# An attention and mixture-of-experts chain on one core: the order of the opening's ropes, of the zeros' transfers and of the jobs' hand-overs

## The chip, the cores and the metric

The kernel runs on one core of a Trainium2 chip. The core has five engines with a program each: TensorE (PE; matmuls and transposes, with the weight loads, PEld, beside them), VectorE (DVE), ScalarE (ACT), GpSimd (POOL) and SyncE (SP), which here only issues transfers (DMA). Each engine works through its own instructions in order and waits for others by semaphores. The metric is the device time of one execution in microseconds (us); lower is better.

## The reference

Three layers in a row, all in float32 as seen from outside; w_in and w_out come as float64 and are turned into float32 pairs on the chip.

```python
q_rot, k_rot = rotate(q), rotate(k)                    # rope; 2 batches, 8 heads, 576 tokens, 64 wide
scores = scale * q_rot @ k_rot.T
attn = exp(scores - max); attn /= sum(attn)
x = (attn @ v), as 1152 tokens x 512

expert = argmax(x @ w_gate)                            # 8 experts, at most 288 tokens kept for each
out[i] = gate_w[i] * (relu(x[i] @ w1[expert]) @ w2[expert])   # 512 -> 1024 -> 512; dropped tokens are 0

h = out @ w_in                                         # 512 -> 2048
g = max(h, 0) + alpha * min(h, 0)
result = g @ w_out                                     # 2048 -> 512
```

## The kernel before, in words

The order of all work is written out by hand (`tc.manual_schedule()`): each engine executes its instructions in the order in which the Python code emits them, and the framework adds the waits. So a call that is moved in the code moves its instructions on every engine that it uses, and nowhere else.

**Attention** (`attention`) works on eight pairs of heads, j = 0 to 7. For a pair it loads k, q and v (`prep_load`), rotates k and q (`ropeA`: three tensor_tensor instructions, two products and a sum; `remA`: the same for the last 64 of the 576 tokens), splits them into a high and a low half (`ropeB`: a rounding on ScalarE and a subtraction; `remB`), transposes them (`prep_T`, `prep_rem`) and copies the result crosswise by DMA (`prep_X`, tile X). `S_step(j, t, hh)` is a block of scores: matmuls on TensorE, the row maximum on VectorE (tile nm), the exponential on ScalarE (tile P). `T_step` transposes a P, and ScalarE or VectorE copies it out of PSUM (tile PT); `AV_steps` multiplies by v (av, then oT). Pair 0 goes a shorter way without halves: `first_T` transposes its rotated q or k for one head (tiles fT, then first), `first_rem` its last 64 tokens (frem). `warm(k)` issues k matmuls on zeros whose result nobody reads. V is VectorE, Q is GpSimd in these calls; H0 and H1 are the first and the second head of the pair. The opening, up to the loop over n at line 501, is a list of such calls; the loop does ten steps n for a pair, and `hook(n)` at the end of a step does other layers' work.

**Zeros.** From n = 17 on, `hook` issues one transfer of zeros (96 x 3 x 512 floats, 576 KB) in each step: nine into x_disp, the buffer of dispatched tokens, and four into out. They go through SP's queue, like the loads of q, k and v and the copies into X. `prep_load(j + 3)` stands in the last step of a pair, so k of pair 5 is loaded at n = 29 and rotated by GpSimd at n = 30.

**The experts** are taken by size (rank r = 0, 1, ...). The first two (r < NSTAT) are done by `job`, in nine steps s: 24 matmuls a step, half of them to h (relu, then split by ScalarE into a high and by VectorE into a low half), half into the four accumulators acc. Between these, `job(r)` splits its own weights and those of rank r + 1 (`split`: ScalarE rounds, VectorE subtracts; tiles wraw to whl), issues the loads of rank r + 1 on SP (`load`, `load_xs`), and transposes rank r + 1's tokens (`turn_x`, `make_xT`; tiles xs, xt, then split_room or x32). `job(1)` also splits the first float64 weights of the last layer (`split_w_in`, five instructions for each quarter; tiles rawy and room) and loads the next ones (`load_w_in`). After the two jobs the program branches; the way taken here (`short_way`) does ranks 2, 3 and 4 in float32 with `mid_job` (160 columns) and `small_job` (32 columns each), in which `next_x` turns the next rank's tokens and loads those of the one after. Before the change the fourth rank's tokens (r = 3) are loaded at the start of `mid_job`, behind the loads of rank 3's second and third weights.

**The last layer** (`ffn`) then runs over three blocks of 272, 256 and 256 columns, and the results are scattered to out by GpSimd.

Of the kernel before, what the change touches and what calls it, by code (L numbers as in the profile page):

```python
# [37 lines left out]
NSTAT = 2  # L38
WS = 192
USE = (0, 2, 1, 3)  # L40
SIZES = (32, 64, 128, 160, 192, W)
FIT = (W, W, 160, 32, 32)
# [21 lines left out]
def attention(nc, tc, q, k, v, wg, tab, rtab, x_tok, lp, ident, idr, hook):  # L64
# [3 lines left out]
    with ExitStack() as ctx:  # L68
# [372 lines left out]
        H0, H1 = (0, 1), (1, 2)  # L441
# [5 lines left out]
        ropeA(0, Q, 1, H1)  # L447
        remA(0, V)
        first_T(1, 0)
        first_T(0, 0)  # L450
# [6 lines left out]
        remA(1, Q)  # L457
        first_T(0, 1, nc.vector)
        T_step(0, 0, 0)
        S_step(0, 2, 0)  # L460
        prep_sums(1)
        ropeA(1, Q, 0)
        S_step(0, 0, 1)
        prep_load(2)
        remB(1, V)
        ropeB(1, Q, 1)
        ropeA(2, Q, 1)
        T_step(0, 0, 1)
        ropeB(1, V, 0)
        T_step(0, 1, 0)  # L470
        T_step(0, 2, 0)
        prep_load(3)
# [9 lines left out]
        T_step(0, 3, 0)  # L482
        prep_T(1, 0, 1)
        T_step(0, 2, 1)
# [363 lines left out]
def build(nc, tc, cap, q, k, v, wg, w1, w2, w_in, w_out, alpha, tab, rtab, out):  # L848
    assert 0 < cap <= W
    with ExitStack() as top:  # L850
# [113 lines left out]
        def hook(n, psum):  # L964
# [12 lines left out]
            if n > 16 and fill:  # L977
                nc.sync.dma_start(fill.pop(0), zero[0:96].unsqueeze(1).broadcast_to([96, 3, 512]))
# [24 lines left out]
        with ExitStack() as ctx:  # L1003
# [235 lines left out]
            with ExitStack() as c1:  # L1239
# [45 lines left out]
                def job(r, base, nxt):  # L1285
# [13 lines left out]
                    for s in range(9):  # L1299
# [40 lines left out]
                        for chore in chores.pop((r, s), ()):  # L1340
                            chore()
                        if r < NSTAT:
                            if s in ((0, 1) if r else (1, 2)):
                                split(r, 2, ((0, 1), (2, 3))[s - (r == 0)], lo)
                            if s in (3, 4):
                                split(r, 3, part, lo)
                            if s in (2, 5) and nxt:
                                load(r + 1, 2 + s // 4)
# [16 lines left out]
                        if nxt:  # L1365
# [4 lines left out]
                            for c in ({3: (0,), 5: (1,), 6: (2,), 7: (3,)} if r else {6: (0, 1), 7: (2, 3)}).get(s, ()):  # L1370
                                if r + 1 == NSTAT:
                                    nc.scalar.copy(x32[:, c], turn_x(r + 1, c, ph, "xt")[:, 0:WS])
                                    continue
                                src = make_xT(r + 1, c, ph, "xt")
                                if r + 1 > NSTAT:
                                    nc.vector.tensor_copy(x32[:, c], src[:, 0:WS])
# [8 lines left out]
                        if r == 1 and s in (2, 4):  # L1385
                            load_w_in(1, 2 - s // 2)
# [73 lines left out]
                def mid_job(r, base, nxt, n, nx=None):  # L1460

                    h = [h32[:, f * n : f * n + n] for f in range(8)]
                    if nxt and r == NSTAT:
                        load_xs(r + 1, nx or n)
# [84 lines left out]
                for r in range(NSTAT):  # L1549
                    job(r, None if r else 0, True)  # L1550
                load(NSTAT + 1, 2)
# [110 lines left out]
```

## Time and profile before

| | us |
|---|---|
| median of three runs | 418.86 |
| the three runs | 418.72, 422.13, 418.86 |
| the profiled execution, its own time | 422.35 |
| its span, first to last instruction | 420.6 |
| mean granted TensorE clock in it | 0.989 |

| engine | busy us | share of the span |
|---|---|---|
| TensorE | 394.2 | 94% |
| VectorE | 284.6 | 68% |
| ScalarE | 225.4 | 54% |
| GpSimd | 137.2 | 33% |

TensorE is busy nearly all the time. So the place to read is not the share of an engine but the places where TensorE waits, and for each of them which engine or transfer ended the wait. The profiled execution is one execution, and its own time is nearer to the slowest of the three runs than to their median.

### The profile page before, as it was taken

To read this page: it belongs to the slowest core of one execution; us is meant where nothing else is said; L and a number is where in the kernel's file an instruction comes from. 1 tells how busy PE (TensorE), PEld (TensorE's weight loads), DVE (VectorE), ACT (ScalarE), POOL (GpSimd) and SP (SyncE) were. 2 spreads that over 40 slices of the span, in tenths; PEclk is the share of its full clock that TensorE was granted. 3 is DMA by queue.
4 is the path that set the end of the run, shared out by engine and by line. 5 is a ranking of instruction groups with operands and counts; after the bars stand their busy time and mean duration, and the time that the engine had idled before them with its cause. 6 is when DMAs were issued, how large, how long until landed. Compare 5 with 4: busy or idle time off the path is not lost. (4 is left out here: it accounts for less than half of the span.)

```text
span 420.6 us, 8109 instructions
## 1 busy us (share of the span) xinstructions
PE 394.2 (94%) x2999; PEld 334.9 (80%) x2999; DVE 284.6 (68%) x643; ACT 225.4 (54%) x565; POOL 137.2 (33%) x180
## 2 busy tenths in 40 slices
PE   5899999989999999999898889899999999999994
PEld 2577888777978777799798887699799789879873
DVE  6566566465877465688698802199999999983621
ACT  7587787578867687447634411176327415622500
POOL 5899594499496333250000071000000000000032
PEclk9799999999999999999999999999999999999998
DMA  7622999905023631857957598940550253000022
GB/s 211 167 60 61 165 349 303 275 7 133 1 58 114 207 106 46 292 182 244 319 183 265 200 316 270 397 158 2 200 201 2 70 201 132 2 0 2 0 77 81
DMA packets 37328, 63.70 MB, mean 151 GB/s; under 512 B 9886, under 2 KB 16158, under 8 KB 37280
## 3 DMA queue, kind: packets, MB, share of 16 engines
q1 hardware_dynamic: 35424, 58.83, 44.1%
q0 software_dynamic: 1568, 3.95, 2.6%
q8 instruction: 25, 0.41, 0.4%
q10 hardware_dynamic: 288, 0.33, 0.2%
q14 instruction: 23, 0.19, 0.1%
HBM read 47.35 MB, written 11.65 MB: 140 GB/s over the span
## 5 line engine op out<-in xcount | busy, mean ns | idle before, releaser
L309 DVE TENSOR_REDUCE nm<-S 128x1 f32<-128x576 f32 x72 | 54.2, 753 | 39.0 <-ACT PT L320 20.6
L1135 PE MATMUL u_a<-yh,whl 128*128 128x256 f32 (+1 forms) x576 | 71.1, 284 | 0.6 <-ACT yh L1457 0.4
L1135 PEld LDWEIGHTS u_a<-yh,whl 128*128 128x128 f32 x576 | 70.1, 188 | 1.8 <-ACT room L1145 0.9
L310 ACT ACTIVATE P<-S,nm 128x576 f32<-128x576 f32 x72 | 53.7, 746 | 24.5 <-DVE nm L309 23.1
L596 POOL DMA_INDIRECT out<-xs,room x3 | 2.9, 974 | 150.3 <-DVE xs L1211 150.3
L331 PE MATMUL pt<-ident,P 128*128 128x128 f32 x256 | 39.0, 277 | 3.6 <-ACT P L310 2.0
L1199 PE MATMUL acc<-whl,split_room 128*128 128x512 f32 x162 | 41.5, 392 | 0.0
L1029 ACT CAST whl<-wraw 128x512 fp32r<-128x512 f32 x22 | 14.6, 662 | 48.9 <-DVE wraw L1027 48.9
L300 PE MATMUL S<-T,T 128*128 128x288 f32 x112 | 36.4, 341 | 1.2 <-ACT P L310 0.9
L1199 PEld LDWEIGHTS acc<-whl,split_room 128*128 128x128 f32 x162 | 29.9, 188 | 9.4 <-issue 2.6
L320 ACT COPY PT<-pt 128x512 f32<-128x512 f32 x64 | 35.4, 557 | 2.2 <-PE pt L331 2.2
L331 PEld LDWEIGHTS pt<-ident,P 128*128 128x128 f32 x256 | 28.7, 141 | 8.9 <-ACT P L310 3.7
L363 PE MATMUL av<-PT,v 128*64 128x288 f32 x256 | 34.8, 412 | 0.0
L1199 PE MATMUL acc<-whl,g 128*128 128x512 f32 x126 | 32.6, 390 | 0.0
L300 PE MATMUL S<-X,T 128*128 128x288 f32 x112 | 31.2, 293 | 0.0
L1146 DVE SCALAR_TENSOR_TENSOR room<-room,nal 128x256 f32<-128x256 f32 (+1 forms) x48 | 23.4, 487 | 8.9 <-ACT room L1145 8.7
L1199 PEld LDWEIGHTS acc<-whl,g 128*128 128x128 f32 x126 | 23.5, 188 | 5.7 <-issue 0.9
L596 POOL DMA_INDIRECT meta_d<-g_meta,m_mi x10 | 9.6, 961 | 56.1 <-DVE m_mi L839 53.4
L1144 ACT ACTIVATE room<-u_a 128x256 f32<-128x256 f32 (+1 forms) x48 | 19.0, 396 | 15.5 <-PE u_a L1135 15.5
L363 PEld LDWEIGHTS av<-PT,v 128*64 128x64 f32 x256 | 17.2, 136 | 12.0 <-issue 1.9
L300 PEld LDWEIGHTS S<-T,T 128*128 128x128 f32 x112 | 21.1, 188 | 3.0 <-ACT P L310 2.5
L136 POOL TENSOR_TENSOR A<-raw,tabt 128x512 f32<-128x512 f32 (+1 forms) x15 | 19.1, 1276 | 9.5 <-DMA raw<-k 9.1
(288 smaller groups left out, 853.5 us busy)
## 6 DMA issues: line engine op xcount, KB each, us to landing
wraw<-moe_w SPq DMA_DIRECT2D x16, 1024.0 KB, 7.0
wraw<-moe_w_out SPq DMA_DIRECT2D x3, 2048.0 KB, 8.1
x_disp<-zero SPq DMA_DIRECT2D x9, 576.0 KB, 7.2
wraw<-moe_w_in SPq DMA_DIRECT2D x2, 2048.0 KB, 7.5
X<-T SPq DMA_DIRECT2D x14, 288.0 KB, 5.5
room<-moe_w SPq DMA_DIRECT2D x3, 1024.0 KB, 7.6
out<-zero SPq DMA_DIRECT2D x4, 576.0 KB, 7.8
v<-v SPq DMA_DIRECT2D x8, 256.0 KB, 4.4
```

The costliest lines, as they stand in the source:

```text
L136: eng.tensor_tensor(A, raw, bc(C), op=ALU.mult)
L300: nc.tensor.matmul(ps[:, half, 0:288], lhsT=lhsT, rhs=rhs, start=(n == 0), stop=(n == len(terms) - 1),)
L309: nc.vector.tensor_reduce(nm, ps[:, :, 0:288], op=ALU.max, axis=AX.XY, negate=True)
L310: nc.scalar.activation(Pt.rearrange("p (a n) -> p a n", a=2), ps[:, :, 0:288], AF.Exp, bias=nm, scale=1.0, accum_out=st["ssum"][:, t, hh : ...
L320: (nc.vector.tensor_copy if SCH["e"][k] else nc.scalar.copy)(o, i)
L331: nc.tensor.transpose(ps[:, kb, :], Pt[:, at : at + 128], ident)
L363: nc.tensor.matmul(ps[64 * hh : 64 * hh + 64, 0:288], lhsT=lhs, rhs=(PT[:, hh, kb] if kb < 4 else PR)[:, half * 288 : half * 288 + 288], s ...
L1029: nc.scalar.copy(ht[:, 0, c], hw.bitcast(F32))
L1135: nc.tensor.matmul(ps, lhsT=wt[:, a, c, (f % 4) * 128 : (f % 4) * 128 + 128], rhs=yh_[0][:, b, c, c0 + lo : c0 + hi], start=(c == 0 and i ...
L1144: nc.scalar.activation(A, ps, AF.Relu)
L1146: nc.vector.scalar_tensor_tensor(A, Bn, nal[:, f : f + 1], A, op0=ALU.mult, op1=ALU.add)
L1199: nc.tensor.matmul(ps[:m], lhsT=g_cols(g, b, t * P, t * P + m), rhs=wt[:, a, c, :], start=(c == 0 and i == 0), stop=(c == 3 and i == 2),)
```

## The change

In the opening the second half of pair 0's k goes from GpSimd to VectorE, behind the rope of the remaining tokens (`remA(0, V)`); two warm matmuls are added; GpSimd's `remA(1, Q)` and the order of some transposes and copies change. The zeros are issued at every second step. In `job`, the next rank's tokens are transposed and copied ahead of the splits and loads of the same step, and the second load of float64 weights goes ahead of the other loads. The load of rank 3's tokens goes from the start of `mid_job` to the end of the second job, ahead of two weight loads.

```diff
         ropeA(0, V, 1, H0)
         ropeA(0, V, 0, H0)
-        ropeA(0, Q, 1, H1)
         remA(0, V)
         first_T(1, 0)
+        ropeA(0, V, 1, H1)
+        warm(2)
         first_T(0, 0)
         first_rem()
         S_step(0, 0, 0)
...
         S_step(0, 1, 0)
-        remA(1, Q)
         first_T(0, 1, nc.vector)
         T_step(0, 0, 0)
         S_step(0, 2, 0)
+        remA(1, Q)
         prep_sums(1)
         ropeA(1, Q, 0)
+        prep_load(2)
         S_step(0, 0, 1)
-        prep_load(2)
         remB(1, V)
         ropeB(1, Q, 1)
         ropeA(2, Q, 1)
+        T_step(0, 1, 0)
+        ropeB(1, V, 0)
+        prep_load(3)
+        T_step(0, 2, 0)
         T_step(0, 0, 1)
-        ropeB(1, V, 0)
-        T_step(0, 1, 0)
-        T_step(0, 2, 0)
-        prep_load(3)
...
         T_step(0, 3, 0)
+        T_step(0, 2, 1)
         prep_T(1, 0, 1)
-        T_step(0, 2, 1)
...
-            if n > 16 and fill:
+            if n > 16 and n % 2 and fill:
                 nc.sync.dma_start(fill.pop(0), zero[0:96].unsqueeze(1).broadcast_to([96, 3, 512]))
...
                         for chore in chores.pop((r, s), ()):
                             chore()
+                        if nxt:
+                            for c in ({3: (0,), 5: (1,), 6: (2,), 7: (3,)} if r else {6: (0, 1), 7: (2, 3)}).get(s, ()):
+                                if r + 1 == NSTAT:
+                                    nc.scalar.copy(x32[:, c], turn_x(r + 1, c, ph, "xt")[:, 0:WS])
+                                    continue
+                                src = make_xT(r + 1, c, ph, "xt")
+                                if r + 1 > NSTAT:
+                                    nc.vector.tensor_copy(x32[:, c], src[:, 0:WS])
                         if r < NSTAT:
...
+                            if r == 1 and s in (2, 4):
+                                load_w_in(1, 2 - s // 2)
                             if s in (2, 5) and nxt:
                                 load(r + 1, 2 + s // 4)
...
-                            for c in ({3: (0,), 5: (1,), 6: (2,), 7: (3,)} if r else {6: (0, 1), 7: (2, 3)}).get(s, ()):
-                                if r + 1 == NSTAT:
-                                    nc.scalar.copy(x32[:, c], turn_x(r + 1, c, ph, "xt")[:, 0:WS])
-                                    continue
-                                src = make_xT(r + 1, c, ph, "xt")
-                                if r + 1 > NSTAT:
-                                    nc.vector.tensor_copy(x32[:, c], src[:, 0:WS])
...
-                        if r == 1 and s in (2, 4):
-                            load_w_in(1, 2 - s // 2)
...
-                    if nxt and r == NSTAT:
-                        load_xs(r + 1, nx or n)
+                    if nxt and r == NSTAT and nx is None:
+                        load_xs(r + 1, n)
...
                     job(r, None if r else 0, True)
+                load_xs(NSTAT + 1, FIT[NSTAT + 1])
                 load(NSTAT + 1, 2)
                 load(NSTAT + 1, 1)
```

What stands in the engines' programs, first on VectorE in the opening, before. A, B and R are a rope's two products and its sum, remA, remB and remR those of the remaining tokens, nm the row maximum of the first scores:

```order
L136 TENSOR_TENSOR A_0_215<-raw_0_169,tabt 128x256
L137 TENSOR_TENSOR B_0_216<-raw_0_169,tabt 128x256
L139 TENSOR_TENSOR R_0_217<-A_0_215,B_0_216 128x4x64
L136 TENSOR_TENSOR remA_224<-rem,rtabt 64x256
L137 TENSOR_TENSOR remB_225<-rem,rtabt 64x256
L139 TENSOR_TENSOR remR_226<-remA_224,remB_225 64x256
L184 COPY first<-frem 64x64
L186 TENSOR_SCALAR first<-frem 64x64
L309 TENSOR_REDUCE nm_0_0_253<-S_0_0_249 128x1
```

The same place on VectorE now (raw_0_167 is k, raw_0_169 is q):

```order
L136 TENSOR_TENSOR A_0_215<-raw_0_169,tabt 128x256
L137 TENSOR_TENSOR B_0_216<-raw_0_169,tabt 128x256
L139 TENSOR_TENSOR R_0_217<-A_0_215,B_0_216 128x4x64
L136 TENSOR_TENSOR remA_221<-rem,rtabt 64x256
L137 TENSOR_TENSOR remB_222<-rem,rtabt 64x256
L139 TENSOR_TENSOR remR_223<-remA_221,remB_222 64x256
L136 TENSOR_TENSOR A_0_209<-raw_0_167,tabt 128x256
L137 TENSOR_TENSOR B_0_210<-raw_0_167,tabt 128x256
L139 TENSOR_TENSOR R_0_211<-A_0_209,B_0_210 128x4x64
L184 COPY first<-frem 64x64
L186 TENSOR_SCALAR first<-frem 64x64
L309 TENSOR_REDUCE nm_0_0_256<-S_0_0_252 128x1
```

The three instructions of k's second head came in behind remR; they were the first three ropes on GpSimd, which now begins with those of pair 1.

On ScalarE at the end of the first job, before. xt_0 to xt_3 are the next rank's tokens in PSUM, whl the rounded weights, h_7 the last step's h, yh the result:

```order
L926 CAST whl_2105<-wraw_2103 128x1024
L946 CAST split_room<-xt_0_2836 128x288
L946 CAST split_room<-xt_1_2842 128x288
L1314 ACTIVATE split_room<-h_7_2848 128x288
L1517 ACTIVATE yh<-ident 128x496 x2
L926 CAST whl_2488<-wraw_2487 128x1024
L946 CAST split_room<-xt_2_2943 128x288
L946 CAST split_room<-xt_3_2949 128x288
L926 CAST whl_2488<-wraw_2487 128x1024
```

The same place on ScalarE now:

```order
L947 CAST split_room<-xt_0_2836 128x288
L947 CAST split_room<-xt_1_2842 128x288
L927 CAST whl_2108<-wraw_2106 128x1024
L1315 ACTIVATE split_room<-h_7_2851 128x288
L1519 ACTIVATE yh<-ident 128x496 x2
L947 CAST split_room<-xt_2_2943 128x288
L947 CAST split_room<-xt_3_2949 128x288
L927 CAST whl_2491<-wraw_2490 128x1024 x2
```

Each pair of tokens' pieces went ahead of the weights' rounding of the same step; VectorE's subtractions moved with them.

On SP in the second job and at its end, before (raw weights of the experts: wraw, and room and rawy once they are free; float64 weights: rawy and room from moe_w_in; COMPARE_AND_BRANCH is the branch to the short way):

```order
L919 DMA wraw_2103<-moe_w 128x4x512
L1037 DMA rawy<-moe_w_in 128x2x1024
L1037 DMA room<-moe_w_in 128x2x1024
L919 ISA
L919 DMA wraw_2487<-moe_w 128x4x512
L919 ISA
L919 DMA room<-moe_w 128x4x512
L919 ISA
L919 DMA room<-moe_w 128x4x512
L919 ISA
L919 DMA rawy<-moe_w 128x4x512
L1635 COMPARE_AND_BRANCH
```

And now, from the same load of float64 weights to the fourth rank's tokens (xs):

```order
L1038 DMA rawy<-moe_w_in 128x2x1024
L920 ISA
L920 DMA wraw_2106<-moe_w 128x4x512
L1038 DMA room<-moe_w_in 128x2x1024
L920 ISA
L920 DMA wraw_2490<-moe_w 128x4x512
L920 ISA
L920 DMA room<-moe_w 128x4x512
L934 ISA
L934 DMA xs<-x_disp 96x512
L920 ISA
L920 DMA room<-moe_w 128x4x512
```

The first float64 load changed places with a weight load, and the tokens, which were issued after the branch, stand ahead of the last two weight loads.

## Rows read from the trace of the kernel before

**Rows 1.** Stretches: us, busy us (count) of PE, PEld, DVE, ACT, POOL; PEclk, DMA, GB/s.

```profile
40.00:60.00 20.00, 19.96 (x170) 16.19 (x164) 11.50 (x25) 15.04 (x38) 15.39 (x21) 1.00 0.97 245
60.00:100.00 40.00, 37.86 (x316) 31.25 (x317) 23.86 (x50) 29.00 (x72) 27.00 (x31) 1.00 0.63 182
```

**Rows 2.** Waits of TensorE: tile, line <- releaser: us in total, times, longest.

```profile
PE pt L331 <- ACT P L310: 2.0, 2, 1.7
PE frem L255 <- DVE remR L139: 2.0, 1, 2.0
PE xs L1269 <- DMA xs<-x_disp: 1.7, 1, 1.7
PE acc L1327 <- DVE split_room L1315: 1.6, 2, 1.2
PE pt L331 <- ACT oT L320: 1.2, 1, 1.2
PE h L1306 <- DVE split_room L947: 1.0, 1, 1.0
PE pT L198 <- POOL hl L162: 0.9, 1, 0.9
...
PE h L1306 <- ACT split_room L946: 0.7, 1, 0.7
```

**Rows 3.** Stretches of TensorE alone in the opening: us, busy (count), PEclk, DMA, GB/s.

```profile
8.00:9.00 1.00, 0.00 (x0) 0.73 1.03 284
...
15.00:16.00 1.00, 1.00 (x9) 0.85 0.07 23
```

**Rows 4.** Timeline of the opening: start, us, engine, line, operation, [idle before <-releaser].

```profile
1.98 3.62 PE L269 MATMUL warm<-x_tok 128*128 128x512 bf16 x9 [1.98 <-DVE x_tok L872]
...
5.53 0.42 DVE L137 TENSOR_TENSOR B<-raw,tabt 128x256 f32<-128x256 f32 x1
...
6.33 0.95 DVE L136 TENSOR_TENSOR remA<-rem,rtabt 64x256 f32<-64x256 f32 x1
...
7.94 0.78 POOL L139 TENSOR_TENSOR R<-A,B 128x256 f32<-128x256 f32 x1
8.18 0.83 DVE L139 TENSOR_TENSOR remR<-remA,remB 64x256 f32<-64x256 f32 x1
...
8.92 1.26 POOL L136 TENSOR_TENSOR A<-raw,tabt 128x512 f32<-128x512 f32 x1 [0.19 <-DMA raw<-k]
...
9.46 2.29 PE L300 MATMUL S<-first 128*128 128x288 f32 x4
...
18.27 1.26 POOL L139 TENSOR_TENSOR R<-A,B 128x512 f32<-128x512 f32 x1
...
20.99 0.62 ACT L161 CAST hl<-R 128x512 fp32r<-128x512 f32 x1
...
24.21 1.20 PE L300 MATMUL S<-first 128*128 128x288 f32 x4
```

**Rows 5.** Timeline around the zeros: the SP queue, and GpSimd's rope of pair 5.

```profile
57.90 0.50 SPq L229 DMA_DIRECT2D X<-T  x1
...
64.37 5.59 SPq L978 DMA_DIRECT2D out<-zero  x3
70.01 1.91 SPq L105 DMA_DIRECT2D raw<-k  x1
...
79.28 1.29 POOL L136 TENSOR_TENSOR A<-raw,tabt 128x512 f32<-128x512 f32 x1 [6.62 <-DMA raw<-k]
```

**Rows 6.** Timeline at the end of the first job and in the second.

```profile
204.79 1.05 ACT L926 CAST whl<-wraw 128x1024 fp32r<-128x1024 f32 x1 [2.32 <-DMA wraw<-moe_w]
...
207.08 0.81 DVE L947 TENSOR_TENSOR split_room<-xt,split_room 128x288 fp32r<-128x288 f32 x2
...
226.86 0.43 DVE L1025 TENSOR_SCALAR cv<-rawy 128x512 uint32<-128x512 uint32 x1 [0.85 <-DMA rawy<-moe_w_in]
```

**Rows 7.** Timeline: the issue of the fourth rank's tokens.

```profile
242.81 0.35 SPq L933 DMA_DIRECT2D xs<-x_disp  x1
```

## The prediction

> **What bounds the kernel now.** I read the stretches first. TensorE is busy 19.96 of the 20 us from 40 to 60 and 37.86 of the 40 us from 60 to 100 [rows 1]. So a microsecond saved ahead of such a stretch reaches its end, and what can be saved is where TensorE waits. The list of its waits [rows 2] names the places, and the change goes to most of them: 2.0 us for the remaining tokens' rope (frem) and 2.0 us for exponentials (one of 1.7), both in the opening; 1.2 and 0.9 us in the attention, behind ScalarE and GpSimd; 0.7 and 1.0 us for the second job's x and 1.6 us (one wait of 1.2) for VectorE inside that job; 1.7 us for the fourth rank's x (xs). Then I read the clock: in the stretch from 8 to 9 us its granted level falls from 1.00 (2.4 GHz) to 0.50 (1.2 GHz), after TensorE had little to do, and in the stretch from 15 to 16 it comes back [rows 3].
>
> **The opening.** Before, VectorE runs the remaining tokens' rope while GpSimd runs the second half of k. VectorE alone takes 0.42 us for 256 columns; beside GpSimd the same size takes 0.95 to 0.83, the three from 6.33 to 9.01 [rows 4]. With k's half taken off GpSimd, that engine has nothing until the k of the next pair lands, which it met at 8.92 with 0.19 of waiting. So the three should take 3 x 0.42 = 1.27 us and end near 7.65, 1.4 us earlier; the three added ropes follow by 8.95, about where GpSimd had ended them (7.94 + 0.78), so the transposes that need them lose nothing. The two added warm matmuls (3.62 / 9 = 0.4 us each) hold TensorE between two transposes; q's transposes move back by some 0.4 us, hidden because ScalarE still clears zeros then. I estimate the first score matmuls at 8.2 instead of 9.46: 1.26 us. Those four took 2.29 us on the low clock, and four of the same take 1.20 on the full one [rows 4]; with TensorE busy from 7.65 on I expect no fall: 1.09 us more. The first row maximum on VectorE then comes some 2.3 us earlier, and the rope of q's second half behind it keeps its price, since GpSimd runs beside it as before. The new order of the transposes puts two that are ready ahead of one that waits 1.7 us for its exponential; I estimate 0.7 of it. The edits left over cost nothing: GpSimd's remA(1) changes places with a memset, prep_load(2) and (3) with nothing on SP, T_step(0, 2, 1) with transposes that are as ready as it is.
>
> Not all of these 3 us arrive. GpSimd's ropes of the next pair start at 8.92 because of the transfer and end at 18.27 + 1.26 = 19.53, and neither moves. ScalarE rounds that q at 20.99 [rows 4]; it cannot before 19.53, and its copies and exponentials are queued behind. That is 1.45, plus what its later idle time gives back. The bounds are 1.4 and 3.0; I take 2.0, nearer to the row that holds it. An execution without the fall has 1.1 of that already, and gains 0.8 to 0.9.
>
> The Trainium skill (SBUF — State Buffer, Who interferes with whom) says that a VectorE instruction with two inputs in SBUF and a GpSimd instruction reading SBUF exclude each other, the first to start holding the port to its end. The rows of 0.42 and 0.95 agree. It also speaks against this change: the added ropes have two such inputs. By the rule, if GpSimd's next rope landed in them, each would take 0.95 and 1.6 of the 2.0 us would be lost; by the rows GpSimd, at 8.92, meets only the end of the last one, and the 2.0 stand.
>
> **The zeros.** Thirteen transfers of 576 KB fill the SP queue, one each step, and nothing but the queue paces them: issuing three takes 5.59 us, then k of pair 5 is issued at 70.01, and GpSimd's rope on it starts at 79.28 after 6.62 us of idling [rows 5]. The rounding on ScalarE waits for that rope, its copies wait behind it, and TensorE stands 1.2 + 0.9 us [rows 2]. With zeros at every second step the diff leaves three ahead of that k instead of six. The X's two halves, issued from 57.90, the three zeros and that k are 2 x 288 + 3 x 576 + 256 KB, 2.6 MB; at the 245 GB/s that the stretch from 40 to 60 averaged [rows 1] that takes 10.6 us, so k lands by 68.5, some 4 us ahead of GpSimd's need at 72.66 (79.28 less 6.62). The zeros moved back come ahead of k of pair 6, again three, and that one is needed a whole pair later. So the wait goes whole, and nothing is late next but ScalarE's ordinary roundings. Bounds 0 and 2.1; I take 2.0.
>
> **The jobs.** At the end of the first job ScalarE waits 2.32 us for a weight transfer with x's pieces 2 and 3 queued behind [rows 6]; TensorE needs them and stands 0.7 + 1.0 us [rows 2]. With x first these 1.7 us of TensorE go. But in the second job TensorE waits for VectorE's low halves (the 1.6 us), and VectorE itself idles 0.85 us for float64 weights [rows 6]. VectorE's work there starts with that same weight transfer at 204.79, which x's place does not move; only its two subtractions on x (0.81) leave the time after it, worth some 0.65 (it can't begin before ScalarE's two roundings). The 0.85 is removed by the other edit: rawy's load goes ahead of a 1 MB load (it can start no earlier than before, since it waits for VectorE to release the buffer) and so no longer shares the queue with it: 1 MB is 4 us at 245 GB/s. Together 1.5; bounds 0 and the 1.7 + 1.6 of TensorE's waits there; I take 1.2. Of the jobs beyond rank 2 only the short way's small and middle ones run, and their order is unchanged.
>
> **The fourth x.** It is issued at 242.81 [rows 7], behind two loads of 1 MB that were held until VectorE released their buffers, and TensorE waits 1.7 us for it. Now it stands ahead of them, issued as soon as TensorE has turned the x before it, which the matmuls ahead of 242.81 already use. The wait goes. The loads behind it are not held, since they wait for VectorE in either order. What follows are loads that TensorE itself releases, so they move with it. Bounds 0 (should those loads bind at once) and 1.7; I take 1.5.
>
> **Sum.** 2.0 + 2.0 + 1.2 + 1.5 = 6.7, from the profiled execution's 422.35: 415.65. Its time is 3.49 over the median of 418.86 (one of the three runs, 422.13, is like it). Of these 3.49, 1.1 to 1.3 is the fall of the clock, which I take the two quick runs to lack, and I have it in the 6.7; the other 2.25 is in no row that I can name, and I let it stand below both kernels: 415.65 - 2.25 = **413.4**. The same from the median: 418.86 - (0.8 + 2.0 + 1.2 + 1.5) = 413.4.
>
> The Trainium skill (TensorE: Matmul & The Clock Gate, What's actually happening) says that the low clock is the default and activity releases it, and that the moment varies from run to run. The two levels in rows 3 agree. By that rule the fall belongs to some executions only, as I took it; with a fall in every run of before, the sum from the median would be 412.3.
>
> **Rivals.**
> - *The jobs' gain is eaten* by VectorE or by the transfers. For it: VectorE idles little in the second job, and the weight transfers keep their place. Then 1.2 and 1.5 shrink to some 0.4 together: 413.4 + 2.3 = 415.7. Chance 0.20.
> - *The zeros' wait is hidden in the quick runs*, their transfers being faster, so there is nothing to remove. For it: two of the three runs are 3.5 us quicker, in no row that I can name. Against it: k, issued at 70.01, would have to land at 72.66 behind four transfers or more. 413.4 + 2.0 = 415.4. Chance 0.12.
> - *The change does not do what it says*: GpSimd's ropes bind the opening fully, the 2.25 that I could not place was the stalls themselves, and one term of the four is left: 418. Chance 0.14.
> - *Slower.* ScalarE's rounding of the next pair's q now stands ahead of two copies that free TensorE's banks, so each microsecond by which GpSimd ends later than 19.53 costs one. VectorE's instructions go from 0.42 to 0.95 beside GpSimd; were GpSimd's 10.6 us (8.92 to 19.53) to stretch alike, by 2.3, they would end 13.4 us later, and 413.4 + 13.4 = 427. It decides from 5.5 us, a stretch of 1.5. Against it: GpSimd's 0.78 for 256 columns beside VectorE is 1.24 times half its 1.26 for 512 [rows 4]. Chance 0.03.
> - *The median has the fall too*, or TensorE gains at the jobs all that it waited: 411.5. Chance 0.06.
>
> **How the numbers follow.** All terms arriving has the rest, 0.45, with a range of its own from 411.5 to 415. From 411 to 418 all cases but the slower one, half of the third rival and the outer edges are held, about 0.85. Faster by over 1% means under 414.67, about what a measurement of this kernel can tell from none: 0.41 of the likeliest, 0.06 of the last, and 0.08 from the first two rivals: 0.55. Slower than 423.05 has 0.03. The rest, 0.42, lies within 1%.
>
> **What would show it.** The opening: VectorE's three instructions on rem at 0.42 us and no stretch of 0.50 between 8 and 15 us. If they still take 0.9, the port was not the reason. The zeros: no wait of GpSimd on raw<-k over 1 us, no wait of TensorE for oT and hl. The jobs: no wait of h for split_room, VectorE without the 0.85, the second job shorter by about 1. The fourth x: no wait of xs on its transfer, and the first matmuls of the third job behind it some 1.5 us earlier relative to that job's start. The prediction is wrong if these waits go and the end does not move, or if a new wait stands at the weight transfers from 255 to 270.

## The result, and the profile after

Five runs of the changed kernel took 413.34 to 415.6 us, median 413.7; the kernel before beside it had a median of 420.7 (five runs, the three known ones among them). The ratio of the two is 0.9896, with a 95% interval of 0.9858 to 0.9934. That is 4.4 us by the ratio, 2.8 to 6.0 by its interval; the means of the same runs differ by 5.9 us and their medians by 7.0, so five runs on either side do not say more than that. Predicted were 413.4 and a ratio of 0.987 (413.4 / 418.86). The profiled execution took 415.6; the sum for it had been 415.65. The total came out; the sections below show that its terms mostly did not, and that one thing that decides the total was in none of the rivals.

The stretches and TensorE's waits first, after the change (columns as in [rows 1, 2]):

```profile
40.00:60.00 20.00, 19.96 (x170) 16.42 (x168) 11.49 (x25) 15.59 (x39) 15.39 (x22) 1.00 0.77 166
60.00:100.00 40.00, 39.64 (x332) 32.81 (x327) 24.15 (x50) 30.15 (x74) 28.57 (x32) 1.00 0.77 229
```

```profile
PE fT L247 <- DVE R L139: 2.5, 1, 2.5
...
PE acc L1328 <- DVE yh L1392: 1.2, 1, 1.2
PE acc L1434 <- DMA room<-moe_w: 1.1, 1, 1.1
```

TensorE's 2.1 us of waiting between 60 and 100 (1.2 for oT, 0.9 for hl) are gone, and so are frem's 2.0, h's 1.7 and xs's 1.7. Three waits are new or larger: 2.5 us in the opening for VectorE's rope of q's second half, 1.2 in the second job, and 1.1 at the weights of the last small job, the place that the prediction had named as the one that would make it wrong.

The opening after, the same instructions as in [rows 4] (timeline: start, us, engine, line, operation, idle time before):

```profile
6.32 0.41 DVE L136 TENSOR_TENSOR remA<-rem,rtabt 64x256 f32<-64x256 f32 x1
...
8.86 1.27 POOL L136 TENSOR_TENSOR A<-raw,tabt 128x512 f32<-128x512 f32 x1 [5.01 <-DMA rem<-k]
...
8.97 1.24 PE L300 MATMUL S<-first 128*128 128x288 f32 x4 [0.41 <-ACT first L182]
...
11.56 1.48 DVE L137 TENSOR_TENSOR B<-raw,tabt 128x256 f32<-128x256 f32 x1
...
13.07 0.95 DVE L139 TENSOR_TENSOR R<-A,B 128x256 f32<-128x256 f32 x1
...
14.08 0.66 PE L247 MATMUL fT<-ident,R 128*128 128x128 f32 x4 [2.46 <-DVE R L139]
...
15.29 3.51 PE L300 MATMUL S<-first 128*128 128x288 f32 x8
```

The remaining tokens' rope takes 0.41 instead of 0.95, and the first four score matmuls run on the full clock (1.24 us instead of 2.29): so far as predicted. They start at 8.97, where the prediction had estimated 8.2. Then q's second half takes 0.71 + 1.48 + 0.95 = 3.1 us beside GpSimd, where it had taken 2.3 in the trace of before:

```profile
12.46 0.57 DVE L136 TENSOR_TENSOR A<-raw,tabt 128x256 f32<-128x256 f32 x1
...
13.93 0.83 DVE L139 TENSOR_TENSOR R<-A,B 128x256 f32<-128x256 f32 x1
```

TensorE stands 2.46 us for it, and its clock falls behind that wait (after the change; us, busy, PEclk, DMA, GB/s, as in [rows 3]):

```profile
8.00:9.00 1.00, 0.59 (x6) 1.00 0.87 235
14.00:15.00 1.00, 0.92 (x7) 0.85 0.78 272
15.00:16.00 1.00, 1.00 (x5) 0.50 0.04 12
```

The eight score matmuls at 15.29 run at 1.2 GHz and take 3.51 us. The fall has moved from 8 to 15 us to 14 to 18 and is half as long; it has not gone.

The zeros, the jobs and the fourth x (timeline; the answers to [rows 5 to 7]):

```profile
63.48 1.89 SPq L105 DMA_DIRECT2D raw<-k  x1
...
73.19 1.28 POOL L136 TENSOR_TENSOR A<-raw,tabt 128x512 f32<-128x512 f32 x1
...
202.07 2.00 ACT L927 CAST whl<-wraw 128x1024 fp32r<-128x1024 f32 x2 [1.46 <-DMA wraw<-moe_w]
...
222.49 0.42 DVE L1026 TENSOR_SCALAR cv<-rawy 128x512 uint32<-128x512 uint32 x1
...
230.37 0.35 SPq L934 DMA_DIRECT2D xs<-x_disp  x1
```

k of pair 5 is issued at 63.48 instead of 70.01 and GpSimd does not wait for it; ScalarE's wait for the weight transfer is 1.46 instead of 2.32, and x's pieces now stand ahead of it instead of behind; VectorE does not wait for rawy; the fourth x is issued at 230.37 instead of 242.81.

**Stretches of every profiled execution.** One trace proved a poor witness, so the rest rests on this table, worked out from all of them: the time from the start of one instruction to the start of another. A: from the start to VectorE's fifth row maximum (opening). B: from the 31st to the 37th (k of pair 5). C: from the 55th to the 61st. D: from ScalarE's eighth Relu in the jobs to the first of the middle job (second job). E: from the middle job's fifth Relu to the first small job's (fourth x). F: from there to the last layer's third (of those on the positive part). "Late" is how long after the end of a matmul its semaphore rose, at worst, for matmuls that ended between 120 and 135 us / between 240 and 256 us ("-": nothing over 0.3), with TensorE's signals matched to its matmuls in order. The names are those of the experiments below.

| kernel | A | B | C | D | E | F | late |
|---|---|---|---|---|---|---|---|
| before | 22.5 | 15.5 | 12.8 | 38.7 | 16.9 | 16.1 | 1.7 / 4.8 |
| after | 23.1 | 13.8 | 11.9 | 37.3 | 13.6 | 17.0 | - / - |
| open_only | 22.7 | 14.6 | 11.8 | 39.2 | 15.4 | 18.3 | - / - |
| zeros_only | 24.1 | 13.8 | 11.9 | 39.4 | 17.0 | 15.8 | - / - |
| jobs_only | 23.3 | 14.2 | 11.8 | 37.2 | 15.3 | 18.7 | - / - |
| xs_only | 21.8 | 13.8 | 11.8 | 39.3 | 13.6 | 22.0 | - / - |
| after_again | 21.3 | 13.8 | 12.8 | 37.4 | 18.3 | 16.7 | 1.7 / 6.5 |
| q_gps | 21.7 | 13.8 | 12.6 | 37.3 | 18.2 | 15.8 | 1.4 / 6.5 |
| warm_fill | 21.8 | 13.8 | 12.8 | 37.4 | 16.8 | 17.5 | 1.8 / 6.5 |
| late_out | 22.9 | 13.8 | 12.9 | 37.3 | 16.8 | 17.6 | 1.8 / 6.5 |
| after_third | 23.1 | 13.8 | 12.9 | 37.0 | 17.0 | 15.8 | 1.7 / 6.5 |
| no_xs | 23.9 | 13.8 | 12.8 | 37.4 | 17.3 | 15.7 | 1.7 / 4.9 |
| meta_late | 22.8 | 13.8 | 12.9 | 37.4 | 13.6 | 16.0 | 1.7 / - |
| meta_ffn | 23.0 | 13.8 | 11.9 | 37.5 | 13.6 | 15.8 | - / - |

The experiments ran on three chips: the four single parts on one, the next seven runs (after_again to meta_late) on a second, meta_ffn on a third. Which chips the traces of before and after come from is not recorded.

### The profile page after: what moved, and what is told of

Same layout as the page of the kernel before. It is cut to its first block, busy times and chain, and to the rows that moved or that the text cites. A ratio compares the mean times of both kernels' runs of the same rounds, so it can differ in the third digit from the quotient of the medians.

```text
span 413.9 us, 8111 instructions
## 1 busy us (share of the span) xinstructions
PE 393.9 (95%) x3001; PEld 335.8 (81%) x3001; DVE 285.7 (69%) x646; ACT 225.4 (54%) x565; POOL 134.4 (32%) x177
## 5 line engine op out<-in xcount | busy, mean ns | idle before, releaser
L331 PE MATMUL pt<-ident,P 128*128 128x128 f32 x256 | 39.2, 279 | 1.3 <-ACT P L310 1.0
L363 PEld LDWEIGHTS av<-PT,v 128*64 128x64 f32 x256 | 17.3, 137 | 12.0 <-issue 1.9
L162 POOL TENSOR_TENSOR hl<-R,hl 128x512 fp32r<-128x512 f32 x12 | 15.3, 1271 | 23.1 <-ACT hl L161 23.0
```

What stands on the lines that cost most here:

```text
L162: eng.tensor_tensor(hl[:, :, 1, :], rv, hl[:, :, 0, :].bitcast(F32), op=ALU.subtract)
L331: nc.tensor.transpose(ps[:, kb, :], Pt[:, at : at + 128], ident)
L363: nc.tensor.matmul(ps[64 * hh : 64 * hh + 64, 0:288], lhsT=lhs, rhs=(PT[:, hh, kb] if kb < 4 else PR)[:, half * 288 : half * 288 + 288], s ...
```

## The experiments

**Each part alone.** The kernel before with one part of the change each; the pieces are those of the diff above (here their first lines):

```diff
 open_only: the three pieces of the opening
-        ropeA(0, Q, 1, H1)
+        ropeA(0, V, 1, H1)
+        warm(2)
 zeros_only:
-            if n > 16 and fill:
+            if n > 16 and n % 2 and fill:
 jobs_only: x's loop moved up, and
+                            if r == 1 and s in (2, 4):
+                                load_w_in(1, 2 - s // 2)
 xs_only:
+                load_xs(NSTAT + 1, FIT[NSTAT + 1])
```

> The kernel before with the new order of the opening alone. As predicted, 2.0 us less (0.8 against an execution of before without the fall of the clock), since the remaining tokens' rope is alone on VectorE and the first scores come earlier. By the two traces, none of it is left: the first score matmuls do come 1.5 us earlier, but the rope of q's second half on VectorE runs beside GpSimd and takes 3.1 us instead of 2.3, TensorE waits 2.5 us for it, and what was gained is gone by the third row maximum (0.6 us later than in the trace of before). By this second theory the time is within 0.6 us of before, on either side; and the profile has the rope's wait of over 2 us on TensorE again.

> The kernel before with zeros at every second step alone. As predicted 2.0 us less. The two traces show 1.6 us gained at 85 to 89 us, and another 1.1 us at 129 to 132 us that the prediction did not have; if the zeros' new places made the second one too (the transfers that TensorE's neighbours wait for there are others then), this kernel is 2.7 us faster; if it came from something else, 1.6 to 2.0. The rival that the wait is hidden in the quick runs: 0.

> The kernel before with the new hand-overs of the jobs alone (x first, and the float64 weights ahead of a 1 MB load). As predicted 1.2 us less (bounds 0 and 3.3). By the two traces 1.3 at the start of the second job and 0.95 inside it: 2.2 us less. By the rival that transfers eat it: 0.4.

> The kernel before with the fourth rank's tokens issued earlier, alone. As predicted 1.5 us less, the length of the wait. The two traces show 3.3 us gained up to the third job and 0.9 given back behind it, at a weight transfer. If the early transfer also does away with the jam in which, before, TensorE's results from 250.7 to 254.3 us were all signalled only after 255.7, this kernel is 2.4 us faster or more, and the trace has no results signalled over 1 us late there; if that jam came from the place in time of the other changes, 1.5 or less, and the late signals are still there.

Measured, as ratios to before with their intervals: opening 1.000 (0.997 to 1.003), zeros 0.9996 (0.997 to 1.002), jobs 0.994 (0.9915 to 0.996), fourth x 0.997 (0.995 to 1.000). In us of 420.6: 0.0, 0.2, 2.6 and 1.1, each within 1.0 to 1.2. So the two terms of 2.0 us gave nothing that can be measured, and the jobs gave twice their 1.2.

Why the zeros give nothing is in column B. Three of these kernels have the old zeros, and GpSimd still waits for k of pair 5 in each. Its rope there, in open_only and in xs_only:

```profile
78.57 1.27 POOL L136 TENSOR_TENSOR A<-raw,tabt 128x512 f32<-128x512 f32 x1 [5.75 <-DMA raw<-k]
```

```profile
76.56 1.28 POOL L136 TENSOR_TENSOR A<-raw,tabt 128x512 f32<-128x512 f32 x1 [4.55 <-DMA raw<-k]
```

With 5.75 us of waiting there the stretch is 14.6, with 4.55 it is 13.8, as without any wait. Only beyond about 4.5 us does GpSimd's wait reach TensorE, and the profiled execution of before, at 6.62, was the worst of the four. What the edit saves is 1.6 us in that execution and 0.8, 0.3 and 0.0 in the others.

The fourth x alone gains 1.7 us up to the first small job (E 13.6) and loses more than that in F (22.0). Its TensorE waits:

```profile
PE sh L1409 <- issue: 1.3, 1, 1.3
...
PE acc L1432 <- DMA room<-moe_w: 1.2, 1, 1.2
PE acc L1432 <- DMA wraw<-moe_w: 1.2, 1, 1.2
```

These add up to 3.7 us, and the clock falls behind them. This execution, with 421.83, is the slowest of that kernel's twelve, so it shows where the gain can go, not what is usual. The theory that the early transfer itself does away with the late signals fell: none of these four has them, whether x is early or not. Nor is the wait for the last small job's weights (room<-moe_w) the early x's doing: open_only and jobs_only, with x at its old place, have it too (1.2 us each).

Three of these kernels have the old opening, and they correct the reading of it. In xs_only the clock does not fall in the opening, and there q's second half takes 3.3 us and TensorE waits 2.8 us for it, with the old order:

```profile
10.98 1.05 DVE L136 TENSOR_TENSOR A<-raw,tabt 128x256 f32<-128x256 f32 x1
11.95 1.48 DVE L137 TENSOR_TENSOR B<-raw,tabt 128x256 f32<-128x256 f32 x1
...
14.45 0.63 PE L247 MATMUL fT<-ident,R 128*128 128x128 f32 x4 [2.77 <-DVE R L139]
```

The four executions of the old opening have 2.3, 2.9, 2.8 and 3.3 us for that rope and waits of 0.4, 2.0, 2.2 and 2.8; the eight of the new one that leave it on VectorE and put nothing into the wait have 3.1 to 3.9 and 2.5 to 3.2. So the wait was there before the change, and the trace of before, in which the rope came last of the four (12.46 us) and met GpSimd's 64-token ropes instead of its 512-wide ones, hid it. What the change does remove is the early fall of the clock: at 8.5 us in before and zeros_only, in none of the ten executions with the new opening.

**The opening: port or clock.** Two variants of the changed kernel:

```diff
 q_gps:
+        ropeA(0, Q, 0, H1)
         first_rem()
         S_step(0, 0, 0)
-        ropeA(0, V, 0, H1)
 warm_fill:
+        warm(10)
         first_T(0, 1, nc.vector)
```

> The changed kernel with the rope of q's second half moved from VectorE to GpSimd, ahead of the next pair's ropes there. Theory one, the port: the opening's gain was lost because that rope on VectorE, beside GpSimd, takes 3.1 us and TensorE waits 2.5 us for it; then it is done by about 10 us instead of 14, that wait falls under 0.5 us, and the third row maximum comes some 2 us earlier, with 1 to 2 us of it left at the end. Rival, GpSimd's ropes of the next pair bind the opening in any case: they now end 1 to 2 us later, TensorE loses at the next pair's transposes what it gained, and the time is the same or up to 1 us longer.

> The changed kernel with ten more warm matmuls on TensorE, in the 2.5 us in which it waits for the rope of q's second half. Theory two, the clock: the opening lost its gain because the idle time made the granted clock fall to 0.50 behind it (14.70 to 18.11 us in the profile after). Then no 0.50 shows between 10 and 20 us, the eight score matmuls at 15.3 take 2.1 us instead of 3.5, and the median is 0 to 1.4 us less (the quicker runs of the changed kernel may lack the fall already). By the port theory alone: the wait of 2.5 us becomes busy time, and the time is the same within 0.5 us.

Ratios to before: q_gps 0.997 (0.9946 to 0.9997), warm_fill 0.997 (0.994 to 0.9997), the changed kernel itself on that chip 0.9956 (0.9936 to 0.9976). Neither is faster than the changed kernel; q_gps is 1.1 us slower in the mean of twelve runs, at the edge of what can be told. Their profiles say why. In q_gps the first line below is k's second half, now the late one, and the second is the next pair's transposes:

```profile
11.27 0.63 PE L247 MATMUL fT<-ident,R 128*128 128x128 f32 x4 [1.67 <-DVE R L139]
...
21.27 0.54 PE L198 MATMUL pT<-idr,hl 128*128 128x128 f32 x4 [0.83 <-POOL hl L162]
```

q's rope on GpSimd (6.94 to 9.44) makes VectorE's ropes beside it take 0.83 to 0.94 us, and the last of them, beside GpSimd's next rope, takes 1.37. The wait for k's rope is 1.7 us, and TensorE then waits for GpSimd's work for the next pair (hl, 19.95 to 21.22) at 21.27. The rival holds here: without the fall, GpSimd's ropes of the next pair bind the opening. In warm_fill:

```profile
10.96 2.32 PE L269 MATMUL warm<-x_tok 128*128 128x512 bf16 x10
13.98 0.63 PE L247 MATMUL fT<-ident,R 128*128 128x128 f32 x4 [0.70 <-DVE R L139]
...
14.88 2.11 PE L300 MATMUL S<-first 128*128 128x288 f32 x8
...
21.34 0.53 PE L198 MATMUL pT<-idr,hl 128*128 128x128 f32 x4
```

The clock stays, and the eight matmuls take 2.11 instead of 3.51, as the clock theory had it. Of the eight other executions with the new opening seven have a fall between 12 and 20 us; of these two variants none. Column A puts its price at some 1.2 to 1.7 us: 22.9 in the mean of the six with one fall of 3.4 us (22.7 to 23.1), 21.3 in after_again and 21.7 and 21.8 in the two variants without. With the fall gone, the pair's transposes start at 20.83 (after_again) to 21.34, right behind GpSimd's last subtraction: that is the floor. The median of warm_fill is nevertheless that of the changed kernel (420.12 against 420.14), with runs from 418.6 to 423.5; why is open.

**The changed kernel again, and the wait for weights.**

```diff
 late_out:
-                        if (r, c) == (3, 1):
+                        if (r, c) == (4, 0):
                             rows64(rawy, w_out[0:256, :])
-                        if (r, c) == (4, 0):
+                        if (r, c) == (4, 2):
                             rows64(raw2[0][:, 2:4], w_out[256:512, :])
```

> The changed kernel as it is, beside the kernel before on the same chip as the four single parts (which gave, in medians of 12 runs: opening 0.0, zeros -0.5, jobs -2.8, fourth x -1.2, together -4.5 from 420.6). If the parts simply add, 416.1. If each of the single gains was partly eaten by the wait for weights at 255 to 270 us, which the whole change gets past, it is under the sum: 413.5 to 414.5.

> The changed kernel with the two prefetches of float64 output weights in the small jobs issued one step later each (behind the steps 4-0 and 4-2 instead of 3-1 and 4-0). If the new wait of 1.1 us for the fourth small job's weights comes from the DMA engines being shared with these prefetches, it falls under 0.5 us and the time is 0.5 to 1.0 us less. If that load is bound by what was queued ahead of it, the wait stays at 1 us or more and the time is the same; if the late prefetch itself is then waited for in the layer behind, the time is up to 1 us longer.

On this second chip the changed kernel takes 420.14 against 421.88 (0.9956): 1.9 us, not the 4.4 of the first comparison, and neither of the two expected figures. late_out is the same (420.06) and its wait stays:

```profile
PE acc L1434 <- DMA room<-moe_w: 1.2, 1, 1.2
```

So the prefetches behind that load are not what delays it. (The wait itself comes and goes: 0.7 us in after_again, none in after_third, with the same program.) What is different on this chip stands in the last column of the table, and in the waits of after_again:

```profile
PE acc L1483 <- issue: 2.5, 4, 1.1
```

Between 244 and 251 us TensorE's results are finished and their semaphores do not rise. VectorE's copy of the fourth job's x, ready at 244.7 by the end of its transposes, starts 6.5 us later, and TensorE comes to a stand; that it has no free bank left is likely and not shown. TensorE's and VectorE's timeline there:

```profile
244.30 0.43 PE L1270 MATMUL xs<-ident,xs 32*128 32x32 f32 x4
244.66 2.72 PE L1483 MATMUL acc<-cv,wraw 128*128 128x160 f32 x18
248.27 0.30 PE L1483 MATMUL acc<-cv,wraw 128*128 128x160 f32 x1 [0.89 <-issue]
...
251.06 5.11 PE L1483 MATMUL acc<-cv,wraw 128*128 128x160 f32 x26 [1.10 <-issue]
```

```profile
251.19 0.29 DVE L1271 COPY room<-xs 128x128 f32<-128x128 f32 x1 [14.58 <-PE acc L1483]
```

The signals arrive when the DMA engines run dry (us, TensorE busy, PEclk, DMA share, GB/s):

```profile
248.00:250.00 2.00, 1.13 (x4) 1.00 1.04 398
250.00:251.00 1.00, 0.00 (x0) 0.78 0.68 226
251.00:254.00 3.00, 2.94 (x12) 0.50 0.40 35
```

The dry spell reads as their effect and not as their cause, since SP's next load waits 6.0 us for one of these signals and is issued with them:

```profile
251.18 0.34 SPq L934 DMA_DIRECT2D xs<-x_disp  x1
```

GpSimd issues the ten scatters of the tokens' weights from 236.9 to 249.2, one every 1.27 us. In the trace of before, where they end at 253.9, the same copy is late by 4.7 us:

```profile
250.68 0.40 PE L1269 MATMUL xs<-ident,xs 32*128 32x32 f32 x4 [1.66 <-DMA xs<-x_disp]
255.82 0.29 DVE L1270 COPY room<-xs 128x128 f32<-128x128 f32 x1 [14.57 <-PE acc L1481]
```

In all seven executions that are late at this place the copy starts 1.9 to 2.0 us after the last scatter's end. The two theories that follow are that this is what eats the fourth x's gain, and that the scatters are its cause.

**With the late signals, is the early x worth anything, and do the scatters make them?**

```diff
 no_xs: the changed kernel, with
+                    if nxt and r == NSTAT:
+                        load_xs(r + 1, nx or n)
-                load_xs(NSTAT + 1, FIT[NSTAT + 1])
 meta_late: the changed kernel, with
-                    gate.scatter_meta(meta_d, "meta_a")
                     mid_job(2, b_r[2], True, FIT[2], FIT[3])
 ...
                         small_job(r, b_s[r], r == 3, FIT[r], after)
+                    gate.scatter_meta(meta_d, "meta_a")
```

> The changed kernel once more, as the measure for the two beside it on this chip. Two chips so far: on the one where four single parts ran, no profile has TensorE's results signalled late at 245 to 256 us; on the other all four profiles have them, up to 6.7 us late while GpSimd issues its ten scatters and the DMA engines are full, and there the whole change gave 1.8 us (420.1 against 421.9) where the first comparison had shown 5.9 in the mean. If that jam decides, this run with a jam gives 1 to 2.5 us against before, and without one 5 to 7.

> The changed kernel with the fourth rank's tokens issued at their old place. As predicted, 1.5 us more than the changed kernel. If the jam decides: on a chip that has it the early transfer only brings TensorE into the jam sooner (from the middle job to the first small one 18.3 us in the changed kernel, 16.9 in the kernel before, which waits 1.7 us first), so this kernel is the same or up to 2 us faster than the changed one; without a jam it is 1.5 to 2.4 us slower.

> The changed kernel with GpSimd's ten scatters of the tokens' weights issued behind the small jobs, at about 264 us instead of 237 (nothing reads them before the last layer is well under way). If the jam at 245 to 256 us comes from the scatters meeting full DMA engines, the late signals are gone there, and on a chip that has the jam this kernel is 2 to 4 us faster than the changed one. If it comes from the full DMA engines alone, the signals are still late and the time is the same. Without a jam on this chip: the same time within 0.5 us.

The same chip again, and the late signals again. after_third 419.98 (0.995, 0.992 to 0.998), no_xs 418.51 (0.994, 0.992 to 0.996): here no gain of the early x can be seen (0.8 us less without it in the means, which the intervals do not tell from none). E is 17.3 in no_xs, with a wait of 1.7 for x in it, and 16.8 to 18.3 in the five runs with the early x: TensorE comes sooner and stands longer, and in the two with 18.2 and 18.3 the clock falls behind the stand.

meta_late takes 420.0, the same as the changed kernel, but its trace answers the question. E is 13.6, as on the other chips, and the middle job runs through (after_again's PE rows above, in meta_late):

```profile
245.56 0.43 PE L1270 MATMUL xs<-ident,xs 32*128 32x32 f32 x4
245.92 6.79 PE L1483 MATMUL acc<-cv,wraw 128*128 128x160 f32 x48
```

The late signals are at 269 to 278 us now, up to 3.4 us, where the scatters stand (264.60 to 278.6), and the last layer pays for them:

```profile
PE u_a L1136 <- ACT room L1146: 2.1, 2, 1.4
```

The scatters carry the late signals with them; this trace, like the other six of this chip, has late signals at its other two rows of scatters too, at 127 to 131 us and at 183 to 187 (five scatters of tokens each; up to 1.8 and 1.1 us). What was expected of the time did not come, because they are late at the new place as well. And full DMA engines are not needed for it. From 272 to 278 the DMA engines are idle (us, TensorE busy, PEclk, DMA share, GB/s), and the Relu at 278.32 reads results that TensorE finished at 274.9:

```profile
272.00:278.00 6.00, 6.00 (x52) 1.00 0.02 1
```

```profile
278.32 0.40 ACT L1145 ACTIVATE room<-u_a 128x272 f32<-128x272 f32 x1 [1.16 <-PE u_a L1136]
```

While the DMA engines were full, up to 270, no signal was over 0.5 us late. What the places have in common is a row of scatters some 1.3 us apart: at each of them the signals get late (by over 0.3 us) 3 to 6 us after the first scatter of the row. TensorE's signals alone are late: of ScalarE's and VectorE's in before, after_again and meta_late none is over 0.3 us.

**The scatters where the DMA engines are idle.**

```diff
 meta_ffn: the changed kernel; scatters and their two read-backs behind the last layer's first step
                     for f in range(17):
+                        if f == (1 if tag == "a" else 0):
+                            weights()
                         if f < 16:
                             up(f)
```

> The changed kernel with GpSimd's ten scatters (and the two small loads that read what they wrote) behind the first step of the last layer, at about 270 us, where the trace after shows the DMA engines at 0.00 to 0.23 until 290. If late signals need scatters and full DMA engines together, none is over 1 us late between 240 and 290 us, the stretch from the middle job's fifth row of results to the first small job's takes 13.6 us on any chip, and nothing is given back in the layer: on a chip with the jam 3 to 4 us faster than the changed kernel there (420.0), 5 to 6 us faster than before; on a chip without it the time of the changed kernel within 1 us. If the scatters alone do it, the late signals are at 270 to 285 us and the time is that of the changed kernel.

A third chip: 414.91 (412.69 to 415.4, six runs) against 419.92, ratio 0.986 (0.981 to 0.990). Nothing is late from 120 us on. The first scatter and the first small job's weights:

```profile
270.76 1.01 POOL L597 DMA_INDIRECT meta_d<-g_meta,m_mi  x1 [84.70 <-DVE m_mi L840]
```

```profile
260.94 1.07 PE L1440 MATMUL acc<-room,cv 128*32 128x128 f32 x32
```

The 1.1 us for weights, which the changed kernel waits at this place at 262.00, are gone, and F is 15.8 instead of 17.0. That the scatters had caused this wait is not shown: with them at their old place zeros_only, after_third and no_xs lack it too.

This kernel beats before. That it beats the changed kernel as well is not shown: the two were not timed on one chip, and 0.986 (0.981 to 0.990) overlaps 0.990 (0.986 to 0.993). Nor does it settle whether late signals need full DMA engines: this chip shows no late signals at the earlier scatters (124 to 130 and 179 to 186 us) either, where the second chip had them in all seven runs. meta_late's trace answers that, and by it late signals would be expected at 270 to 285 us on such a chip; meta_ffn was not tried there.

## Why the prediction came out, and where it did not

**The number.** 413.4 was predicted and 413.7 measured, and that they meet is luck. The median of before was not 418.86: with five runs it was 420.7, on the first chip of the experiments 420.6 in 35 runs. So the baseline was 1.8 us too low. And the change did not give 5.46 us (418.86 - 413.4): by the medians of that comparison it gave 7.0, by the ratio 4.4, on the second chip 1.9 and 2.1. From 420.6, the same terms would have given 415.1.

**The opening (2.0, or 0.8 without a fall): 0.** The remaining tokens' rope fell to 0.41 us each, as predicted, and the fall at 8 us went. The first scores started at 8.97 instead of the estimated 8.2 (8.1 to 9.0 in the ten executions with the new opening). The step that failed is "with TensorE busy from 7.65 on I expect no fall", together with "the rope of q's second half behind it keeps its price". The price was 2.3 us in the trace of before only. In the other executions it was 2.8 to 3.3 with the old order, and 3.1 to 3.9 with the new: come earlier, that rope meets GpSimd's 512-wide ropes, one of its instructions takes 1.48 us where the same takes 0.41 alone, TensorE waits 2.5 us for it, and the clock falls 6 us later than before instead of not at all. The Trainium skill (SBUF — State Buffer, Who interferes with whom) has a two-input VectorE instruction wait for a GpSimd instruction that holds the port to its end. The trace agrees: 1.48 us from 11.56, beside a GpSimd instruction of 1.33 us that had started at 11.43. I had weighed that rule for the ropes that I added and not for the one that I left. The bound by GpSimd's ropes of the next pair, which the prediction gave as the reason for 2.0 instead of 3, is real and lower: even the execution of the changed kernel without a fall (21.3) gains only 0.6 on the one of the old opening without it (21.8).

**The zeros (2.0): about 0.** The mechanism held: k is there, GpSimd does not wait, column B is 13.8 in every kernel with the new zeros. The size was wrong: 2.0 was taken from one execution, and that wait was the longest of the four seen. The rival "hidden in the quick runs", with 0.12, had the effect right and the runs wrong: the wait was mostly or wholly hidden in three of four profiled executions, and these were not quick (421.67, 419.79 and 421.83 us).

**The jobs (1.2): 2.6 by the times, 1.8 by column D** (39.1 as the mean of before and the three other single parts, 37.0 to 37.5 in every kernel that has the edit). I had found 1.5 and cut it to 1.2 for VectorE; no cut was due. What the times show beyond column D lies within their interval. The rival that had this gain eaten was wrong.

**The fourth x (1.5): 1.1 alone, and it depends.** The wait went: without late signals or a fall of the clock, E is 15.3 and 15.4 with the old x and 13.6 with the early one. In after and in xs_only 1.1 us and more come back at the weights of the last small job; open_only and jobs_only wait for these too, so it is open what delays them. Where the late signals are, no gain of the early x can be seen.

**What no term held.** The trace of before has late signals (4.8 us at worst around 250 us, 1.7 at 130), that of after has none. So a part of the distance between the two traces is not the change's: 1.0 us in C, and 1.5 of the 3.3 in E (16.9 in before, 15.4 with the old x and no late signals; the 17.0 of zeros_only has a fall of the clock in it, at 250.8 to 254.3 us). It explains the other coincidence, 415.65 and 415.6: column A lost 0.6, B gave 1.6, the end of the first job (between C and D) 0.9, D 1.4, C and E gave 1.0 + 3.3 with the late signals in them, and F took back 0.9: 6.7. The 2.25 us that the prediction could place in no row may be these signals (an estimate: 1.0 + 1.5); no run shows that the quick runs of before lacked them. The four single parts sum to 3.9 us, the whole gave 4.4 (2.8 to 6.0) in one comparison and 1.9 and 2.1 in two others on the chip with the late signals.

**What stays open.** Why signals are late on one chip of three, with the same program, and by which path scatters delay them. Each time a row of scatters was being issued; full DMA engines are not a condition.

## What to carry to other kernels

A wait that is read from one profiled execution is a bound on the gain, not the gain: look at a second execution, or at how far the wait is from not mattering (here 4.5 of 6.6 us were free), before it becomes a term. When work is taken off one of two engines that share a port, follow the pair to the next instructions that meet: work that comes earlier meets other instructions, and the price that one trace shows holds for that meeting only. And look at the distance between a matmul's end and its signal before choosing a place for scatters that nothing needs soon: engines that wait for TensorE's results pay for it, whether the DMA engines are full or idle.

## What the runs showed of the hardware

- A matmul's semaphore can rise up to 6.5 us after its end. On the second chip all six runs with the scatters at 237 to 252 us had this (4.9 to 6.5 us), and the seventh had it where the scatters then stood (3.4 us, with DMA engines at 0.02); on the two other chips none of five.
- The lateness at the five scatters of tokens (122 to 131 us) costs 1.0 us of attention: C is 12.6 to 12.9 where it is and 11.8 to 11.9 where it is not.
- A VectorE instruction with two inputs (128x256) took 0.41 us alone and up to 1.49 us beside GpSimd's 512-wide ones (1.26 to 1.53 us).
- Ten matmuls of no use in a wait of 2.5 us left the granted clock at 1.00 in the one trace taken, where seven of eight executions without them had a fall, and the eight matmuls behind took 2.11 us instead of 3.51; the end of the kernel did not show it.
